# Second layer in three blocks of 512 tokens, the reciprocal kept in h's PSUM bank, and a later start for the first weight conversion

## The chip, the core and the metric

The kernel runs on one core of one Trainium2 chip. The metric is the device time of one execution in microseconds (us), and the figure that is compared is the median over several runs. A profile of one execution lies beside it; times within the profile count from the start of its span.

## The reference

Three stages follow each other. A clustered attention over q, k and v (2 batches, 8 heads, 768 tokens, head size 64) gives 1536 tokens of 512 features; a first layer multiplies them by a 512 x 2048 matrix, applies a leaky rectifier and multiplies by a 2048 x 512 matrix; a second layer does the same with a rational function in the place of the rectifier.

```python
def _attn_ref(q, k, v, centroids):
    ...
    mask = q_assign[:, :, :, None] == k_assign[:, :, None, :]
    scores = scale * np.matmul(q, k.transpose(0, 1, 3, 2))
    scores = np.where(mask, scores, -1000000000.0)
    ...
    return np.matmul(attn, v).astype(np.float32)

def _moe_ref(x, w_in, w_out):
    h = x @ w_in
    g = np.maximum(0.01 * h, h)
    return (g @ w_out).astype(np.float32)

def _moe2_ref(x, w_in, w_out, a, b):
    h = x @ w_in
    h2 = h * h
    h3 = h2 * h
    P = a[0] + a[1] * h + a[2] * h2 + a[3] * h3
    Q = 1.0 + np.abs(b[0]) * np.abs(h) + np.abs(b[1]) * h2
    g = P / (Q + 1e-06)
    return (g @ w_out).astype(np.float32)
```

The weights arrive as 64-bit floats, so each has to be turned into a 32-bit float on the chip before it is used.

## The kernel before, in words

Each fp32 operand is split into a high part (`xh`, `wih`, `woh`, `gh`) and a low part (`xl`, `wil`, `wol`, `gl`), and each product is made of three matmuls: high by high, high by low, low by high.

**Attention** runs in 96 units of 128 query rows (`run`, line 770 and after); a pair of heads has `UP` = 12 units. In the loop's step i, PE transposes the probabilities of unit i-4 (`trans_p`, L627) and then computes the scores of unit i+1 (`scores`, L583); ACT copies the transposed high part (`hi`, L640) and computes the exponential (`exp`, L603); DVE computes the row maximum (`row_max`, L592) and the low part (`lo`, L646); POOL normalizes two units at once in every second step (`normalize`, L619). Pieces that prepare a later pair of heads are put into the same steps by a table (`prep_pieces`): transposes of q and k on PE (`trans`, L243), copies and splits (`split_hi`, L293, and `split_lo`, L298, on POOL), and moves by DMA through SP's queue (`place_a` and `place_b`, L305, out of a tile `hl` with two buffers). The program order is the order on each engine.

Beside the attention runs the conversion of the first layer's first two weight tiles, in tiles called `xst`. In unit 12 their loads are issued on SP's queue (`fill[1].preload(4)`, L885). From unit 15 (`UP + 3`, L846) on, one conversion operation is issued every third unit (`fill[1].step()`): the first is `conv_a` on ACT (L897), which reads the loaded tile, and the two tiles take turns. Then come operations on DVE (L904, L910) and a save (L926).

**The two layers** are one list of steps (n, j, f): n is a group of four tiles of 128 hidden features (the first layer's first group is cut into two of two), j a block of tokens, f the hidden tile within the group. The first layer has 3 blocks of 512 tokens, 48 steps; the second 4 blocks of 384, 64 steps (`width`, L988). A step i does this, in program order:

- `make_h(i)`: 12 matmuls into a PSUM bank `h` (pool `hps`, 4 banks): 4 slices of 128 input features by three products;
- in the second layer, for step i-2: `ratio_recip` on ACT (logarithm `ln`, L1173, and exponential `r`, L1174, which give the reciprocal of the denominator `z`);
- for step i-1: `ratio_act` (ACT writes `y`, the absolute value, L1150, and `u`, L1151; POOL computes `z` in two operations, L1154 and L1157);
- for step i-2: `ratio_end` on DVE (L1180, L1183, L1186), then for step i-1 `ratio_poly` on DVE (L1161, L1162);
- `back`: the matmuls of the output `y` for the steps that `backs(i)` names, into PSUM banks `y0` to `y3` (pool `yps`, 4 banks). In the first layer that is step i-3. In the second, every second step does two at once, i-5 and i-4;
- `next_x`: one piece of the second layer's input is split (ACT L1273, POOL L1274);
- for step i-2: `hi` (ACT, `gh`, L1134) and `lo` (DVE, `gl`, L1139), after which h's bank is free for step i+2;
- `collect`: after the last hidden tile of a block, DVE adds the `y` banks to `acc` in SBUF (L1236) or copies them (L1252); in the second layer's last group the sums are stored by DMA (L1241). In the second layer this comes one step after the `back`, and before `lo`.

`r` of the second layer takes the bank `y3`, since three output banks suffice for 384 tokens. The second layer's input lies in three tiles: `a` (tokens 0 to 767), `b` (768 to 1151) and a tile `c` (the rest), while the first layer used `a` for 1024 tokens and `b` for 512. The lines that matter:

```python
def backs(i):
    ks = [i - LAG] if LAG <= i < M0 + LAG else []
    if i % 2 == 1:
        ks += [k for k in (i - 5, i - 4) if M0 <= k < NS]
    return ks
```

Of the kernel before, what the change touches and what calls it, by code (L numbers as in the profile page):

```python
# [9 lines left out]
F32 = mybir.dt.float32  # L10
# [20 lines left out]
def clustered_attention_moe_moe2(  # L31
# [110 lines left out]
    class Attention:  # L142
# [633 lines left out]
        def run(self, extra, fill):  # L776
# [10 lines left out]
            for i in range(first, NU + TL + 11):  # L787
# [58 lines left out]
                if UP + 3 <= i < NU - 2 * UP and i % 3 == 0:  # L846
                    fill[1].step()
# [140 lines left out]
    def width(m):  # L988
        return 512 if m == 0 else BLK
# [30 lines left out]
    with tc.manual_schedule():  # L1020
# [51 lines left out]
        x1["c"] = [yp.tile([P, NCT, BLK], F32R, name=nm) for nm in ("xhc", "xlc")]  # L1072
# [7 lines left out]
        while weights.waits_for(("wi", 0)):  # L1080
# [3 lines left out]
        LAG = 3  # L1084
        steps = [
            (n, j, f) for n, (m, f0, nf) in enumerate(groups)
            for j in range(NT // width(m)) for f in range(nf)
        ]
        M0 = NG * (NT // width(0)) * NF
# [12 lines left out]
        def tl(nm):  # L1102
            return ew.tile([P, BLK], F32, tag=nm, name=nm)
# [4 lines left out]
        def wide(i):  # L1108
            return width(groups[steps[i][0]][0])

        def make_h(i):
            n, j, f = steps[i]
            wih, wil = weights.get(("wi", n))
            w = wide(i)
            hp = hps.tile([P, 512], F32, tag="h", name="h")[:, 0:w]
            if rational(i):
                (xh, xl), sx = x1["aabc"[j]], slice(j * w if j < 2 else 0, (j * w if j < 2 else 0) + w)
            else:
                (xh, xl), sx = x1["a" if j < 2 else "b"], slice(j % 2 * w, (j % 2 + 1) * w)
# [11 lines left out]
        def hi(i):  # L1131
            d = st[i]
            d["gh"] = gp_.tile([P, 512], F32R, tag="gh", name="gh")[:, 0:wide(i)]
            nc.scalar.copy(d["gh"], d["h"])  # L1134

        def lo(i):
            d = st[i]
            d["gl"] = gp_.tile([P, 512], F32R, tag="gl", name="gl")[:, 0:wide(i)]
            nc.vector.tensor_tensor(d["gl"], d["h"], f32(d["gh"]), op=ALU.subtract)  # L1139
# [26 lines left out]
        def ratio_recip(i):  # L1166
            d = st[i]
            if i == M0:
                r = tl("r")
            else:  # L1170
                r = yps.tile([P, 512], F32, tag="y3", name="r")[:, 0:BLK]
            ln = tl("ln")
            nc.scalar.activation(ln, d["z"], AF.Ln, scale=LNC, bias=lnc)  # L1173
            nc.scalar.activation(r, ln, AF.Exp, bias=lnb, scale=-1.0)  # L1174
            d["r"] = r

        def ratio_end(i):
            d = st[i]
            r = d["r"]
# [16 lines left out]
        def shape(i):  # L1196
            final = rational(i)
            return final, QT if final else NCT, 512

        def back(i):  # L1200
            n, j, f = steps[i]
            nf = groups[n][2]
            final, NO, NW = shape(i)
# [3 lines left out]
            for o in range(NO):  # L1207
                if f == 0:
                    if final and i + nf >= NS and o < 2:
                        cur[o] = hps.tile([P, 512], F32, tag="h", name=f"y{o}")  # L1210
                    else:
                        cur[o] = yps.tile([P, 512], F32, tag=f"y{o}", name=f"y{o}")
# [5 lines left out]
                if i == NS - 1 and o == NO - 1:  # L1218
                    for c in range(2):
                        cs = slice(c * NW // 2, (c + 1) * NW // 2)  # L1220
                        cur[o + 1 + c] = yps.tile([P, 512], F32, tag=f"y{c}", name=f"y{c}")
                        mm3(cur[o + 1 + c][:, 0:NW // 2], [(l, r[:, cs]) for l, r in pairs], True, True)
                else:
                    ends = f == nf - 1 or (i == NS - 2 and o == NO - 1)
                    mm3(cur[o][:, 0:NW], pairs, f == 0, ends)

        def collect(i):
# [4 lines left out]
            final, NO, NW = shape(i)  # L1232
# [5 lines left out]
            def store(o, a, cs=slice(0, NW), queue=nc.sync):  # L1238
                b, t = divmod(j * QT + o, T)
# [7 lines left out]
            if i == NS - 1 - nf or i == NS - 1:  # L1247
                order = [NO - 1] + order[:-1]
            for o in order:
                a = accs[:, (j * NO + o) * NW:(j * NO + o + 1) * NW]  # L1250
# [105 lines left out]
```

## Time and profile before

| | |
|---|---|
| median of 3 runs | 800.63 us (800.05, 800.63, 803.45) |
| profiled execution, its own time | 804.82 us |
| its span, first to last instruction | 803.0 us |
| mean granted TensorE clock | 0.997 of full speed |
| PE (matmul) busy | 782.7 us, 97% |
| DVE, ACT, POOL busy | 82%, 66%, 50% |

The stages in the span: attention to about 270 us, the first layer to about 523 us, the second to the end. A matmul's row shows its modelled duration, which overlaps the next one; the distance from one start to the next is what a matmul takes in a stream. The busy time of an engine counts overlap once. "Granted clock" is the share of full speed that TensorE had in a stretch.

### The profile page before, as it was taken

Reading aid. Unit: us, or ns where it says so; the run is one execution under the profiler, and the core shown is the slowest. Engines: PE = TensorE matmul, PEld = TensorE weight load, DVE = VectorE, ACT = ScalarE, POOL = GpSimd, SP = SyncE. Lnnn points to the kernel's source line nnn. Section 1 sums busy time; section 2 is a strip of 40 time slices with the busy share of each in tenths; the row PEclk is TensorE's granted clock in tenths of the full one; section 3 lists DMA queues with packets and bytes.
Section 4 is the critical chain, followed back from the end, with each engine's and each line's share of the span. In section 5 each row is a group of like instructions: output and inputs, shape, how many; then the busy total and the mean of one; then the engine's idle time right before and its main releaser. Section 6 shows DMA issues by size and latency. Waiting matters only on the chain.

```text
span 803.0 us, 12628 instructions
## 1 busy us (share of the span) xinstructions
PE 782.7 (97%) x4218; PEld 686.2 (85%) x4218; DVE 658.9 (82%) x1202; ACT 527.6 (66%) x1103; POOL 398.9 (50%) x440
## 2 busy tenths in 40 slices
PE   8898999999999999999999999999999999999997
PEld 6697898999888788888888888888899998989996
DVE  7986999988989578877477578768998888888886
ACT  5887988988889554454254246448777667676662
POOL 3875877877675423230041024258656555463441
PEclk9999999999999999999999999999999999999999
DMA  3594662654420233336445444421010101000112
GB/s 101 154 217 99 147 153 75 175 136 94 101 89 1 106 105 129 133 122 220 131 156 184 127 162 129 161 91 40 31 36 27 40 27 40 14 2 0 40 40 79
DMA packets 42112, 78.61 MB, mean 98 GB/s; under 512 B 5248, under 2 KB 25280, under 8 KB 42048
## 3 DMA queue, kind: packets, MB, share of 16 engines
q1 hardware_dynamic: 41760, 77.65, 32.5%
q8 instruction: 33, 0.54, 0.3%
q14 instruction: 31, 0.25, 0.1%
q10 hardware_dynamic: 288, 0.16, 0.1%
HBM read 49.84 MB, written 9.96 MB: 74 GB/s over the span
## 4 chain that ended last, share of the span: by engine, by line
PE 79%; DVE 8%; DMA 4%; ACT 4%; POOL 3%; issue 1%; SPq 0%; DVEq 0%; POOLq 0%; ACTq 0%
PE y L1097 31%; PE h L1097 30%; PE o L663 5%; PE pT L627 5%; PE s L583 5%; DVE pl L646 2%; DVE nm L592 2%; PE sims L326 2%; DMA xst<-in_moe_w_in_dram 1%; ACT ph L640 1%; PE pa L243 1%; POOL e L619 1%; DMA st<-in_moe_w_out_dram 1%; DMA kraw<-in_k_dram 1%; DMA st<-in_moe_w_in_dram 1%
## 5 line engine op out<-in xcount | busy, mean ns | idle before, releaser
L646 DVE TENSOR_TENSOR pl<-pT,ph 128x384 fp32r<-128x384 f32 x192 | 97.2, 546 | 21.0 <-ACT ph L640 20.8
L619 POOL TENSOR_SCALAR e<-e,sum 128x768 f32<-128x768 f32 x96 | 88.6, 935 | 43.1 <-DVE sum L615 31.2
L920 POOL TENSOR_TENSOR wil<-wf,wih 128x512 fp32r<-128x512 f32 x32 | 42.9, 1353 | 128.3 <-ACT wih L917 121.7
L1154 POOL TENSOR_SCALAR z<-y,abv 128x384 f32<-128x384 f32 x64 | 43.1, 674 | 114.8 <-ACT y L1150 114.8
L1139 DVE TENSOR_TENSOR gl<-h,gh 128x384 fp32r<-128x384 f32 (+1 forms) x112 | 67.9, 609 | 35.2 <-ACT gh L1134 35.0
L1097 PE MATMUL h<-xha,wih 128*128 128x512 f32 (+1 forms) x256 | 92.8, 363 | 0.6 <-DVE gl L1139 0.6
L1097 PE MATMUL h<-xha,wil 128*128 128x512 f32 (+1 forms) x256 | 92.8, 362 | 0.0
L1097 PE MATMUL h<-xla,wih 128*128 128x512 f32 (+1 forms) x256 | 92.7, 362 | 0.0
L603 ACT ACTIVATE e<-s,nm 128x768 f32<-128x768 f32 x96 | 87.4, 910 | 7.8 <-DVE nm L592 4.6
L640 ACT CAST ph<-pT 128x384 fp32r<-128x384 f32 x192 | 82.3, 482 | 15.4 <-PE pT L627 13.8
L592 DVE TENSOR_REDUCE nm<-s 128x1 f32<-128x768 f32 x96 | 90.9, 947 | 0.5
L1134 ACT CAST gh<-h 128x384 fp32r<-128x384 f32 (+1 forms) x112 | 59.1, 528 | 41.3 <-DVE h L1186 39.8
L627 PE MATMUL pT<-ident,e 128*128 128x128 f32 x576 | 81.6, 276 | 3.2 <-DVE pl L646 3.1
L910 DVE SCALAR_TENSOR_TENSOR wf<-st,wf 128x512 int32<-128x512 int32 x124 | 80.9, 706 | 0.0
L1097 PE MATMUL y<-woh,gh 128*128 128x512 f32 (+1 forms) x193 | 74.9, 388 | 0.7 <-ACT r L1174 0.7
L1097 PE MATMUL y<-woh,gl 128*128 128x512 f32 (+1 forms) x193 | 75.5, 391 | 0.0
L627 PEld LDWEIGHTS pT<-ident,e 128*128 128x128 f32 x576 | 67.4, 143 | 9.4 <-DVE pl L646 2.6
L1097 PE MATMUL y<-wol,gh 128*128 128x512 f32 (+1 forms) x193 | 75.4, 391 | 0.0
L1097 PE MATMUL y<-gl,woh 128*128 128x512 f32 x192 | 74.9, 390 | 0.1
L1097 PE MATMUL y<-gh,wol 128*128 128x512 f32 x192 | 74.8, 389 | 0.0
L1097 PE MATMUL y<-gh,woh 128*128 128x512 f32 x192 | 74.7, 389 | 0.0
L897 ACT ACTIVATE wf<-st 128x512 f32<-128x512 f32 x62 | 41.4, 669 | 42.3 <-DMA st<-in_moe_w_in_dram 20.5
(131 smaller groups left out, 2045.8 us busy)
## 6 DMA issues: line engine op xcount, KB each, us to landing
st<-in_moe_w_out_dram SPq DMA_DIRECT2D x32, 512.0 KB, 4.4
st<-in_moe_w_in_dram SPq DMA_DIRECT2D x30, 512.0 KB, 4.8
a<-hl SPq DMA_DIRECT2D x56, 192.0 KB, 4.4
b<-hl SPq DMA_DIRECT2D x28, 192.0 KB, 5.7
wf<-scratch_wi SPq DMA_DIRECT2D x14, 256.0 KB, 2.6
qraw<-in_q_dram SPq DMA_DIRECT2D x16, 192.0 KB, 2.8
kraw<-in_k_dram SPq DMA_DIRECT2D x16, 192.0 KB, 3.6
vraw<-in_v_dram SPq DMA_DIRECT2D x8, 384.0 KB, 4.8
```

The costliest lines, as they stand in the source:

```text
L592: nc.vector.reduce_max(un["nm"], un["s"][:, 0:S], axis=AX.X, negate=True)
L603: nc.scalar.activation(un["e"], un["s"][:, 0:S], AF.Exp, bias=un["nm"], accum_out=un["recip"])
L619: nc.gpsimd.tensor_scalar(un["e"], un["e"], un["recip"], 1.0, op0=ALU.mult, op1=ALU.mult)
L627: nc.tensor.transpose(pp[:, kt * P:(kt + 1) * P], un["e"][:, k0:k0 + P], ident)
L640: nc.scalar.copy(un["hi", part], un["pT", part])
L646: nc.vector.tensor_tensor(self.group[gi]["pl"][:, part * n:(part + 1) * n, i * P:(i + 1) * P], un["pT", part], f32(un["hi", part]), op=ALU ...
L910: nc.vector.scalar_tensor_tensor(wi, hold["st", i][:, :, :, 1 - w], sc, wi, op0=op, op1=ALU.bitwise_or)
L920: nc.gpsimd.tensor_tensor(hold["l"][:, i:i + wr, :], hold["wf", i], f32(hold["h"][:, i:i + wr, :]), op=ALU.subtract,)
L1097: nc.tensor.matmul(o, lhsT=l, rhs=r, start=(first and idx == 0), stop=(last and idx == n - 1),)
L1134: nc.scalar.copy(d["gh"], d["h"])
L1139: nc.vector.tensor_tensor(d["gl"], d["h"], f32(d["gh"]), op=ALU.subtract)
L1154: nc.gpsimd.tensor_scalar(d["z"], d["y"], abv[:, 1:2], abv[:, 0:1], op0=ALU.mult, op1=ALU.add)
```

## The change

The second layer gets the first's shape: 3 blocks of 512 tokens, 48 steps, with the input where the first layer had its own (`x_block`; tile `c` is gone). `ratio_recip` writes the reciprocal over `d["h"]`, in h's own bank, and `ratio_end` works there in place; four banks of `y` serve both layers. `backs` gives one step at a time: i-3 for the first layer, i-4 for the second; `collect` follows in the same step, after `lo`. For the very last step the last output tile is made in two halves in banks of `hps`. In attention, `UP + 3` becomes `UP + 6`.

```diff
-                if UP + 3 <= i < NU - 2 * UP and i % 3 == 0:
+                if UP + 6 <= i < NU - 2 * UP and i % 3 == 0:
                     fill[1].step()
...
-    def width(m):
-        return 512 if m == 0 else BLK
+    W = 512
...
-        x1["c"] = [yp.tile([P, NCT, BLK], F32R, name=nm) for nm in ("xhc", "xlc")]
...
         def tl(nm):
-            return ew.tile([P, BLK], F32, tag=nm, name=nm)
+            return ew.tile([P, W], F32, tag=nm, name=nm)
...
+        def x_block(j):
+            return x1["aab"[j]], slice(j % 2 * W, (j % 2 + 1) * W)
...
         def ratio_recip(i):
             d = st[i]
-            if i == M0:
-                r = tl("r")
-            else:
-                r = yps.tile([P, 512], F32, tag="y3", name="r")[:, 0:BLK]
             ln = tl("ln")
             nc.scalar.activation(ln, d["z"], AF.Ln, scale=LNC, bias=lnc)
-            nc.scalar.activation(r, ln, AF.Exp, bias=lnb, scale=-1.0)
-            d["r"] = r
+            nc.scalar.activation(d["h"], ln, AF.Exp, bias=lnb, scale=-1.0)
...
             nc.vector.scalar_tensor_tensor(
-                d["h"], r, -2.0, d["u"], op0=ALU.add, op1=ALU.mult
+                r, r, -2.0, d["u"], op0=ALU.add, op1=ALU.mult
             )
 
         def backs(i):
-            ks = [i - LAG] if LAG <= i < M0 + LAG else []
-            if i % 2 == 1:
-                ks += [k for k in (i - 5, i - 4) if M0 <= k < NS]
-            return ks
+            return [k for k in (i - LAG, i - LAG - 1) if 0 <= k < NS and rational(k) == (k < i - LAG)]
...
                 if f == 0:
-                    if final and i + nf >= NS and o < 2:
-                        cur[o] = hps.tile([P, 512], F32, tag="h", name=f"y{o}")
-                    else:
-                        cur[o] = yps.tile([P, 512], F32, tag=f"y{o}", name=f"y{o}")
+                    cur[o] = yps.tile([P, W], F32, tag=f"y{o}", name=f"y{o}")
...
         def next_x():
             j, o, a = later.pop(0)
...
+            (xh, xl), sx = x_block(j)
+            nc.scalar.copy(xh[:, o, sx], a)
+            nc.gpsimd.tensor_tensor(xl[:, o, sx], a, f32(xh[:, o, sx]), op=ALU.subtract)
...
-            for k in backs(i - 1):
-                if rational(k):
-                    collect(k)
             for k in backs(i):
                 back(k)
             if later:
                 next_x()
...
             for k in backs(i):
-                if not rational(k):
-                    collect(k)
+                collect(k)
```

Three places of the program, as instructions in order. First ACT in attention, before, around the first conversion operation (`xst`), where `sum` is the end of unit 15 and the `ph` behind it belongs to the next step:

```order
L603 ACTIVATE e,sum<-s,nm 128x768
L610 ACTIVATE sum<-sum,eps 128x2
L897 ACTIVATE xst<-xst 128x512
L640 CAST ph<-pT 128x3x128 x2
L246 ACTIVATE x<-pa 128x384
```

And the same stretch of ACT now:

```order
L603 ACTIVATE e,sum<-s,nm 128x768
L610 ACTIVATE sum<-sum,eps 128x2
L640 CAST ph<-pT 128x3x128 x2
L246 ACTIVATE x<-pa 128x384
L603 ACTIVATE e,sum<-s,nm 128x768
L640 CAST ph<-pT 128x3x128 x2
L246 ACTIVATE x<-pa 128x384
L603 ACTIVATE e,sum<-s,nm 128x768
L610 ACTIVATE sum<-sum,eps 128x2
L640 CAST ph<-pT 128x3x128 x2
L676 COPY tmp<-o 64x384
L603 ACTIVATE e,sum<-s,nm 128x768
L897 ACTIVATE xst<-xst 128x512
```

The operation on `xst` stands three units (three exponentials) later; nothing else of ACT moved there.

Second, DVE at the end of a block in the middle of the second layer, before (`acc<-y` is the collection of three output tiles, `gl` the low part, the rows that read `r` are `ratio_end`, the two that write `u` from `h` are `ratio_poly`):

```order
L1186 SCALAR_TENSOR_TENSOR h<-r,u 128x384
L1161 TENSOR_TENSOR u<-u,h 128x384
L1162 SCALAR_TENSOR_TENSOR u<-u,nav,h 128x384
L1236 TENSOR_TENSOR acc<-y_7241,acc 128x512
L1236 TENSOR_TENSOR acc<-y_7245,acc 128x512
L1236 TENSOR_TENSOR acc<-y_7249,acc 128x512
L1139 TENSOR_TENSOR gl<-h,gh 128x384
L1180 SCALAR_TENSOR_TENSOR u<-u,nav,r 128x384
```

And now:

```order
L1176 SCALAR_TENSOR_TENSOR h<-h,u 128x512
L1156 TENSOR_TENSOR u<-u,h 128x512
L1157 SCALAR_TENSOR_TENSOR u<-u,nav,h 128x512
L1134 TENSOR_TENSOR gl<-h,gh 128x512
L1217 TENSOR_TENSOR acc<-y_6861,acc 128x512
L1217 TENSOR_TENSOR acc<-y_6865,acc 128x512
L1217 TENSOR_TENSOR acc<-y_6869,acc 128x512
L1217 TENSOR_TENSOR acc<-y_6873,acc 128x512
L1170 SCALAR_TENSOR_TENSOR u<-u,nav,h 128x512
L1173 SCALAR_TENSOR_TENSOR h<-z,h 128x512
```

The collection stands behind `gl`, has four tiles, and follows its matmuls in the same step; `r` has become `h` in `ratio_end`.

Third, ACT where the second layer begins, now (the exponential L1165 writes `h` where it wrote `r`; `xha<-acc` is the split of the second layer's input):

```order
L1145 ACTIVATE y<-h 128x512
L1146 ACTIVATE u<-h,nav 128x512
L1250 CAST xha<-acc 128x512
L917 CAST wih<-wf 128x512
L1164 ACTIVATE ln<-z,lnc 128x512
L1165 ACTIVATE h<-ln,lnb 128x512
```

Before, a piece of the split was two instructions (of 256 and 256, or 128 and 384 tokens); now it is one of 512, and the exponential's output stands in the bank that `ratio_poly` has read.

## Rows read from the trace of the kernel before

**Rows 1.** The page's busy line: time, share of the span and instructions of each engine.

```profile
PE 782.7 (97%) x4218; PEld 686.2 (85%) x4218; DVE 658.9 (82%) x1202; ACT 527.6 (66%) x1103; POOL 398.9 (50%) x440
```

**Rows 2.** Waits of PE, the longest: who for whom, total us, times, longest.

```profile
PE pa L243 <- DVE pl L646: 3.2, 1, 3.2
```

**Rows 3.** Stretches of first and second layer: length, busy us per engine, granted clock, DMA.

```profile
440.00:480.00 40.00, 40.00 (x179) 33.11 (x178) 24.41 (x39) 15.69 (x27) 5.55 (x4) 1.00 0.47 158
600.00:640.00 40.00, 40.00 (x204) 36.44 (x203) 34.56 (x65) 28.29 (x54) 22.49 (x25) 1.00 0.09 31
```

**Rows 4.** The same view, three stretches of attention (order: PE, PEld, DVE, ACT, POOL).

```profile
58.00:62.00 4.00, 2.23 (x14) 1.73 (x14) 1.91 (x4) 1.01 (x4) 2.77 (x4) 1.00 1.07 282
62.00:66.00 4.00, 2.61 (x14) 2.32 (x15) 3.22 (x7) 4.00 (x10) 0.93 (x1) 0.80 1.06 227
66.00:70.00 4.00, 4.00 (x24) 3.81 (x24) 2.61 (x6) 2.58 (x7) 2.24 (x3) 0.78 0.63 138
```

**Rows 5.** Timeline of ACT, units 15 to 18: start, duration, instruction, wait before it.

```profile
57.44 0.90 ACT L603 ACTIVATE e<-s,nm 128x768 f32<-128x768 f32 x1
...
61.72 0.66 ACT L897 ACTIVATE xst<-xst 128x512 f32<-128x512 f32 x1 [2.96 <-DMA xst<-in_moe_w_in_dram]
...
69.54 0.90 ACT L603 ACTIVATE e<-s,nm 128x768 f32<-128x768 f32 x1
```

**Rows 6.** Timeline of POOL in the same stretch.

```profile
67.76 0.83 POOL L293 TENSOR_SCALAR hl<-x 128x768 fp32r<-128x768 f32 x1 [4.83 <-DMA a<-hl]
68.57 1.80 POOL L619 TENSOR_SCALAR e<-e,sum 128x768 f32<-128x768 f32 x2
```

**Rows 7.** Timeline of PE in the same stretch.

```profile
63.39 0.55 PE L243 MATMUL pa<-ident,kraw 128*128 128x128 f32 x3 [3.17 <-DVE pl L646]
...
73.59 0.82 PE L627 MATMUL pT<-ident,e 128*128 128x128 f32 x6
```

**Rows 8.** Timeline of PE in the first layer, matmuls number 1 and 241 of a stretch.

```profile
397.49 0.39 PE L1097 MATMUL h<-xha,wih 128*128 128x512 f32 x1
...
451.89 0.39 PE L1097 MATMUL h<-xhb,wih 128*128 128x512 f32 x1
```

**Rows 9.** Chain that ended last, second layer: start, us, line, count (pairs 1 and 26).

```profile
566.17 4.18 PE h L1097 x24
570.35 4.12 PE y L1097 x18
...
773.84 4.18 PE h L1097 x24
```

**Rows 10.** Timeline of PE where the second layer begins.

```profile
541.22 0.34 PE L1097 MATMUL h<-xha,wil 128*128 128x384 f32 x1
542.13 0.45 PE L1097 MATMUL h<-xha,wih 128*128 128x384 f32 x1 [0.57 <-DVE gl L1139]
...
560.76 0.34 PE L1097 MATMUL h<-xhb,wil 128*128 128x384 f32 x1
561.81 0.47 PE L1097 MATMUL y<-woh,gh 128*128 128x512 f32 x1 [0.71 <-ACT r L1174]
```

**Rows 11.** Groups of DVE, shapes apart, 300 to 500 us: count, busy us, mean ns.

```profile
L1139 DVE TENSOR_TENSOR gl<-h,gh 128x512 fp32r<-128x512 f32 x37 | 25.2, 686 | 22.9 <-ACT gh L1134 22.8
```

**Rows 12.** The same view, 566 to 790 us, and ACT's there.

```profile
L1139 DVE TENSOR_TENSOR gl<-h,gh 128x384 fp32r<-128x384 f32 x55 | 30.3, 550 | 0.0
L1236 DVE TENSOR_TENSOR acc<-y,acc 128x512 f32<-128x512 f32 x30 | 18.8, 682 | 0.0
L1173 ACT ACTIVATE ln<-z,lnc 128x384 f32<-128x384 f32 x54 | 33.4, 618 | 9.4 <-POOL z L1157 8.5
L1174 ACT ACTIVATE r<-ln,lnb 128x384 f32<-128x384 f32 x55 | 32.2, 586 | 1.8
```

**Rows 13.** Timeline of DVE and PE at the end.

```profile
795.20 0.56 DVE L1139 TENSOR_TENSOR gl<-h,gh 128x384 fp32r<-128x384 f32 x1 [0.60 <-ACT gh L1134]
796.61 2.71 DVE L1236 TENSOR_TENSOR acc<-y,acc 128x512 f32<-128x512 f32 x5 [0.85 <-PE y L1097]
```

More of the change, by code (lines that the diff above doesn't have):

```diff
@@ L1084, in clustered_attention_moe_moe2 @@
         LAG = 3
+        NO = W // P
         steps = [
             (n, j, f) for n, (m, f0, nf) in enumerate(groups)
-            for j in range(NT // width(m)) for f in range(nf)
+            for j in range(NT // W) for f in range(nf)
         ]
-        M0 = NG * (NT // width(0)) * NF
+        M0 = NG * (NT // W) * NF
         NS = len(steps)
@@ L1113, in make_h @@
             wih, wil = weights.get(("wi", n))
[L1114 to L1117, printed above, removed]
-            else:
-                (xh, xl), sx = x1["a" if j < 2 else "b"], slice(j % 2 * w, (j % 2 + 1) * w)
+            hp = hps.tile([P, W], F32, tag="h", name="h")
+            (xh, xl), sx = x_block(j)
             sl = slice(f * P, (f + 1) * P)
@@ L1132, in hi @@
             d = st[i]
-            d["gh"] = gp_.tile([P, 512], F32R, tag="gh", name="gh")[:, 0:wide(i)]
+            d["gh"] = gp_.tile([P, W], F32R, tag="gh", name="gh")
             nc.scalar.copy(d["gh"], d["h"])
@@ L1137, in lo @@
             d = st[i]
-            d["gl"] = gp_.tile([P, 512], F32R, tag="gl", name="gl")[:, 0:wide(i)]
+            d["gl"] = gp_.tile([P, W], F32R, tag="gl", name="gl")
             nc.vector.tensor_tensor(d["gl"], d["h"], f32(d["gh"]), op=ALU.subtract)
@@ L1219, in back @@
                     for c in range(2):
-                        cs = slice(c * NW // 2, (c + 1) * NW // 2)
-                        cur[o + 1 + c] = yps.tile([P, 512], F32, tag=f"y{c}", name=f"y{c}")
-                        mm3(cur[o + 1 + c][:, 0:NW // 2], [(l, r[:, cs]) for l, r in pairs], True, True)
+                        cs = slice(c * W // 2, (c + 1) * W // 2)
+                        cur[NO + c] = hps.tile([P, W], F32, tag="h", name="yh")
+                        mm3(cur[NO + c][:, 0:W // 2], [(l, r[:, cs]) for l, r in pairs], True, True)
                 else:
                     ends = f == nf - 1 or (i == NS - 2 and o == NO - 1)
-                    mm3(cur[o][:, 0:NW], pairs, f == 0, ends)
+                    mm3(cur[o], pairs, f == 0, ends)
         def collect(i):
@@ L1236, in add, with store @@
                 nc.vector.tensor_tensor(a, y, a, op=ALU.add)
-            def store(o, a, cs=slice(0, NW), queue=nc.sync):
-                b, t = divmod(j * QT + o, T)
+            def store(o, a, cs=slice(0, W), queue=nc.sync):
+                b, t = divmod(j * NO + o, T)
                 t = tile_of(t)
@@ L1246, in collect @@
             order = list(range(NO))
-            if i == NS - 1 - nf or i == NS - 1:
+            if i == NS - 1:
                 order = [NO - 1] + order[:-1]
             for o in order:
-                a = accs[:, (j * NO + o) * NW:(j * NO + o + 1) * NW]
+                a = accs[:, (j * NO + o) * W:(j * NO + o + 1) * W]
                 if first:
-                    nc.vector.tensor_copy(a, cur[o][:, 0:NW])
+                    nc.vector.tensor_copy(a, cur[o])
                 else:
-                    add(cur[o][:, 0:NW], a)
+                    add(cur[o], a)
                 if last and not final:
@@ L1259, in collect @@
             if i == NS - 1:
-                a = accs[:, (j * NO + NO - 1) * NW:(j * NO + NO) * NW]
+                a = accs[:, (j * NO + NO - 1) * W:(j * NO + NO) * W]
                 for c in range(2):
-                    cs = slice(c * NW // 2, (c + 1) * NW // 2)
-                    add(cur[NO + c][:, 0:NW // 2], a[:, cs])
+                    cs = slice(c * W // 2, (c + 1) * W // 2)
+                    add(cur[NO + c][:, 0:W // 2], a[:, cs])
                     store(NO - 1, a, cs, (nc.sync, nc.scalar)[c])
@@ L1267, in next_x @@
             j, o, a = later.pop(0)
[L1268 to L1274 removed]
+            (xh, xl), sx = x_block(j)
+            nc.scalar.copy(xh[:, o, sx], a)
+            nc.gpsimd.tensor_tensor(xl[:, o, sx], a, f32(xh[:, o, sx]), op=ALU.subtract)
         later = []
@@ L1280, in load_step @@
             weights.step(max(0, due - (total - weights.pending())))
-        for i in range(NS + LAG + 3):
+        for i in range(NS + LAG + 1):
             if i < NS and steps[i][1:] == (0, 0):
```

21 lines of the change are left out of this document (4 added, 17 removed).

## The prediction

> **What bounds the kernel now.** I read the busy line of the page first. PE works 97% of the span [rows 1], so time is won only where PE stands idle, runs slowly, or needs less time for the same columns. The table by stretches then shows the layers apart from the rest: PE is busy in all 40 us of a stretch of either layer, at full granted clock, while DVE has 61% of the time in the first layer and 86% in the second [rows 3]. Shorter waits inside the layers' steady part are therefore worth nothing; only the distance from one matmul to the next counts. The list of PE's waits shows where it is idle: one wait of 3.2 us stands alone at the top [rows 2]. Its place is in attention near 60 us, and there the granted clock falls as well, to 0.80 and 0.78, which means that part of that time ran at 1.2 in place of 2.4 GHz [rows 4]. Two more waits lie where the second layer begins [rows 10]. The change touches exactly these: the width in the second layer, its beginning, its end, and the spot in attention.
>
> **The second layer's steady part.** In the first layer 240 matmuls of 512 columns take 451.89 - 397.49 = 54.40 us, 0.2267 us each [rows 8]. In the second, 24 of 384 columns take 4.18 us, 0.1742 each, and 18 of 512 columns 4.12 us, 0.2289 each [rows 9]. Twenty-five pairs of steps take 773.84 - 566.17 = 207.67 us, 8.31 us a pair, with no gap. So 128 columns more cost 0.0525 us, and a matmul has a fixed part of some 0.017 us that does not shrink with its width; where widths alternate, the 512-column ones are also 0.0022 us slower than in the first layer.
>
> The change keeps the columns and makes 64 x 12 = 768 matmuls of `h` into 48 x 12 = 576. By these rows `h` falls from 768 x 0.1742 = 133.8 us to 576 x 0.2267 = 130.6 us: 3.2 us. The 576 matmuls of `y` stay, and if all widths are equal each saves 0.0022 us: 1.3 us. By pairs the sum is 32 x 8.31 = 265.9 against 48 x 24 x 0.2267 = 261.2 us. I take 4.6 us. The bounds are 3.2 (the slower `y` was not due to the mixing) and 4.7.
>
> The Trainium skill (TensorE: Matmul & The Clock Gate, section Back-to-back issue gap) gives the warm distance as columns over 2.4 GHz plus 2.5 ns, so that 192 matmuls fewer would be worth 0.5 us, by an estimate from that page. The rows above have 0.2267 us where that gives 0.216, and I hold with the rows.
>
> **Does PE stay fed at 512?** A step now takes PE 24 x 0.2267 = 5.44 us. The old step took 4.15 us, in which DVE was busy 34.56 us in 40, or 3.59 us a step [rows 3], 0.51 of it the three collected tiles per four steps (0.682 each, rows 12). Scaled by 4/3 the rest is at most 4.1 us, and four collected tiles add 0.68: 4.8 us, 88% of a step. One row has the same operation at both widths: `gl` goes from 550 to 686 ns, by 1.25 [rows 11, 12], so 4.8 is the high end. ACT (28.29 us in 40, now at most 3.9 us a step) and POOL (3.1) have more room. So I cost the wider work at nothing; PE covers it. The cover is 0.6 us a step, and if DVE needs more than 5.44 us a step, the excess falls on PE 48 times.
>
> The collection loses its step of delay: DVE must clear bank `y0` before the next block's first `y`. Between lie 12 matmuls of `h`, 2.7 us, and the four adds can follow PE bank by bank, 0.68 us each, so the last ends 0.7 us after PE leaves it. Behind them on DVE waits `ratio_end` of the next step, and behind that the low part that PE needs two steps, 11 us, later. Nothing.
>
> The reciprocal now overwrites `h`, so the exponential (ACT) must wait for `ratio_poly` of its own step (DVE). Queued behind it on ACT are the absolute value and `u` of the next step. On DVE `gl` of the step before, 0.69 us, lies between `ratio_poly` and the first reader of the reciprocal; the exponential takes 0.59 us at 384 and at most 0.78 at 512 [rows 12]. That hides all but a tenth of a microsecond, inside the 0.6 spare. The in-place reading of a PSUM bank is already done on `r` today, so it has no new price. Nothing.
>
> **Where the second layer begins.** PE stands twice: 542.13 - 541.22 - 0.17 = 0.74 us and 561.81 - 560.76 - 0.17 = 0.88 us [rows 10], 1.6 us. The first is a bank of `h` whose low part is late, the sixth step of the second layer. That step starts 18.8 us after the layer's first now, and 24.5 us after it with 512 columns and single `y` steps, while the chain behind it grows by less than 2 us. The second ends when DVE clears `y` banks after a pair of blocks' steps; it will have its 2.7 us. The exponential no longer waits for bank `y3`, and the input's split has 24 instructions on ACT and POOL together in place of 40. Gain 1.6 us, bounds 0 and 1.6.
>
> **The end.** Now PE's last matmuls are followed by adds of DVE and the stores [rows 13]; that stays, with four tiles for three, three of them cleared while PE still works. New is the order before it: after the last `h`, PE has four steps of `y`, 48 x 0.2267 = 10.9 us, and needs the last low part 0.45 us later, at 11.3. DVE first collects a block, which ends at 2.7 + 0.7 = 3.4 us, and then has ten operations to the last `gl`: 10 x 0.69 = 6.9 us at the price of rows 11, and 0.6 of waiting for `gh` as now [rows 13]: 10.9 us. It fits with 0.4 us to spare; if the operations with two constants scale by the full 4/3 it is about a microsecond late. I take a loss of 0.5 us, bounds 0 and 1.
>
> Sum for the second layer: 4.6 + 1.6 - 0.5 = 5.7 us.
>
> **The spot in attention.** ACT waited 2.96 us, to 61.72, for the load of `xst` [rows 5]; everything behind it on ACT, the copies `ph` first, came late, then DVE's `pl`, then PE, idle for 3.17 us [rows 7]. The slow clock cost (1 - 0.80) x 4 + (1 - 0.78) x 4 = 1.7 us of PE's time more [rows 4]. Together 4.9 us. Three units later the operation stands behind the exponential that now starts at 69.54 [rows 5]; without the stall that one comes some 5 us earlier, at about 64.7, ends at 65.5, and the load has been there since 61.7. So the wait goes.
>
> What is late next is POOL: it waited 4.83 us, to 67.76, for a DMA that frees `hl`, and only then normalizes units 16 and 17, from 68.57 [rows 6]. That DMA does not come earlier because ACT does. PE's transposes of unit 16 now start at 73.59 [rows 7]; they can't start before the first normalization ends, 68.57 + 0.90 = 69.5. So 4.1 of the 4.9 us can be kept. The other conversion operations move by three units too, so they stand at the same places of a unit. The two saves on SP's queue pass eight moves out of `hl`; their data are complete two turns of the tile before, so nothing behind them waits. Nothing.
>
> In the profiled execution the sum is 5.7 + 4.1 = 9.8 us: 804.82 - 9.8 = 795.0. That execution is 4.2 us above the median of the runs, and the runs spread by 3.4. The landing of a load in heavy traffic is what can differ from run to run, so the median run may have a smaller stall. I take 3.0 us for it there, ACT's own wait [rows 5], between 0 and 4.9: 800.63 - 5.7 - 3.0 = **791.9 us**.
>
> **Rivals.**
> - *Attention gives nothing in the median* (chance 0.24): the stall is the profiled execution's own, or POOL's wait on the DMA of `hl` [rows 6] takes its place whole. For it speaks the 4.2 us between profile and median. 800.63 - 5.7 = 794.9.
> - *The fixed part of a matmul is not saved* (0.05): `h` then costs as much per column as before, and 3.2 us drop out: 795.1. Rows 8 and 9, with both widths in one trace, speak against it. It is the outcome that the page of the Trainium skill named above comes near to.
> - *DVE sets the pace* (0.06): the exponential is not hidden behind `gl`, because ACT reaches logarithm and exponential only after `ratio_poly`. A step on DVE is then 4.8 us plus the two at 4/3 of 0.62 and 0.59 [rows 12], 1.6: 6.4, and 48 x (6.4 - 5.44) = 46 us are lost: 800.63 - 8.7 + 46 = 838. It decides from a step of 5.44 us on, and outweighs the gain from 5.62. Against it: `z` is ready long before, and the logarithm needs nothing else.
> - *Smaller gains, no change that can be told* (0.05): the beginning keeps its waits and the end loses a microsecond, with nothing from attention: 800.63 - 4.6 + 1 = 797.0.
>
> **Numbers.** The forecast has 0.60. Its own range is 789.0 to 794: the low end has the whole of attention and no loss at the end, 800.63 - 6.2 - 4.9 = 789.5, with half a microsecond of run to run. The first two rivals carry the range up to 796.6. A measurement of this kernel can tell about 0.5%, 4 us. Faster than 796.6: the forecast, most of the first two rivals, 0.84. Same: 0.10. Slower: 0.06.
>
> **What would show it.** Right: in the second layer, starts of matmuls 0.2267 us apart and steps of 5.44 us; no wait of PE over 0.3 us between its first and last step; DVE's share below 90%; no wait of ACT on `xst`, and the granted clock at 1.00 near 60 us, with a PE wait of about a microsecond in front of unit 16. Wrong: a wait of PE for `gl` or `acc` in every block, a step longer than 5.44 us, or the 3 us stall found again at another place of attention.

## The result, and the profile after

The changed kernel takes 794.46 us (median of 6 runs, 793.58 to 794.83), the kernel before 800.76 (6 runs, 799.92 to 804.02) beside it. The ratio is 0.9911, its 95% interval 0.9891 to 0.9932: faster, and clear of the 0.5% that the prediction took as the least that can be told. The forecast was 791.9, so the sign is right and the point is 2.6 us too low. 794.46 lies half a microsecond above the forecast's own range (789.0 to 794) and inside the wider one up to 796.6, which its first two rivals carry; it is the first rival's 794.9 that the time comes nearest to. The new profiled execution takes 794.29 us, its span 792.2, at a granted clock of 1.000. The two profiled executions thus differ by 804.82 - 794.29 = 10.5 us, where the prediction's sum had 9.8. The medians differ by 6.3, where it had 8.7. What is to be explained is this gap between profile and median.

The page's busy line after, which answers to [rows 1]:

```profile
PE 775.4 (98%) x4026; PEld 658.6 (83%) x4026; DVE 646.2 (82%) x1106; ACT 510.7 (64%) x1015; POOL 387.8 (49%) x400
```

The 192 matmuls are gone (4218 to 4026), and so are 96 instructions of DVE and 88 of ACT. PE is now busy for 98% of a shorter span.

The table by stretches after: three pieces of attention (against [rows 4]) and two of the second layer (against [rows 3]):

```profile
58.00:62.00 4.00, 4.00 (x27) 3.44 (x27) 3.97 (x8) 3.79 (x9) 2.77 (x4) 1.00 1.09 243
62.00:66.00 4.00, 4.00 (x33) 3.90 (x32) 3.78 (x8) 3.74 (x10) 0.14 (x2) 1.00 1.10 209
66.00:70.00 4.00, 3.87 (x27) 3.34 (x27) 3.08 (x7) 3.52 (x11) 4.00 (x5) 1.00 0.70 142
560.00:600.00 40.00, 40.00 (x179) 33.11 (x178) 34.31 (x52) 26.47 (x43) 21.21 (x20) 1.00 0.10 34
600.00:640.00 40.00, 40.00 (x178) 33.15 (x177) 35.29 (x54) 26.66 (x44) 23.20 (x22) 1.00 0.12 40
```

Near 60 us PE worked 2.23 and 2.61 us of 4 before, at a clock down to 0.78. Now it works all of the time, at 1.00. In the second layer 178 or 179 matmuls stand in 40 us where 204 stood; DVE is busy 34.3 and 35.3 us, 86 and 88%.

The longest waits of PE after (us in total, times, longest), where [rows 2] had the wait for `pa` at the top:

```profile
PE pT L627 <- DVE pl L646: 3.4, 7, 1.1
PE s L583 <- ACT e L603: 2.6, 8, 0.7
```

The 3.2 us before `pa` are gone, and between 500 and 790 us no wait of PE is left at all, so those of [rows 10] are gone as well. The chain that ended last, from the last steps of the first layer to the last `h`:

```profile
531.92 2.72 PE y L1096 x12
534.64 5.44 PE h L1096 x24
540.08 2.72 PE y L1096 x12
...
771.28 2.72 PE h L1096 x12
```

Twelve matmuls take 2.72 us without a break, so a step takes 5.44 us and a matmul 0.2267, as in the first layer [rows 8]. The 24 `h` at 534.64 are the one place where a step has no `y`, because `y` then comes one step later.

### The profile page after: what moved, and what is told of

Read it like the earlier page. It is cut to its first block, busy times and chain, and to the rows that moved or that the text cites. A ratio compares the mean times of both kernels' runs of the same rounds, so it can differ in the third digit from the quotient of the medians.

```text
span 792.2 us, 11944 instructions
## 1 busy us (share of the span) xinstructions
PE 775.4 (98%) x4026; PEld 658.6 (83%) x4026; DVE 646.2 (82%) x1106; ACT 510.7 (64%) x1015; POOL 387.8 (49%) x400
## 4 chain that ended last, share of the span: by engine, by line
PE 83%; DVE 9%; POOL 3%; ACT 3%; issue 1%; DMA 0%; DVEq 0%; POOLq 0%; ACTq 0%
PE h L1096 33%; PE y L1096 31%; PE o L663 5%; PE s L583 5%; PE pT L627 4%; DVE pl L646 3%; DVE nm L592 3%; PE sims L326 2%; POOL e L619 2%; ACT ph L640 1%; PE pa L243 1%; ACT e L603 1%; DVE acc L1217 1%; POOL xla L703 0%; DVE sv L357 0%
## 5 line engine op out<-in xcount | busy, mean ns | idle before, releaser
L1129 ACT CAST gh<-h 128x512 fp32r<-128x512 f32 x96 | 56.4, 588 | 69.4 <-DVE h L1176 67.9
L1096 PE MATMUL h<-xha,wil 128*128 128x512 f32 x256 | 99.6, 389 | 0.0
L1096 PE MATMUL h<-xla,wih 128*128 128x512 f32 x256 | 99.6, 389 | 0.0
L1096 PE MATMUL h<-xha,wih 128*128 128x512 f32 x256 | 99.6, 389 | 0.0
L1134 DVE TENSOR_TENSOR gl<-h,gh 128x512 fp32r<-128x512 f32 x96 | 65.6, 686 | 35.7 <-ACT gh L1129 35.4
L1149 POOL TENSOR_SCALAR z<-y,abv 128x512 f32<-128x512 f32 x48 | 37.0, 771 | 117.3 <-ACT y L1145 117.3
L603 ACT ACTIVATE e<-s,nm 128x768 f32<-128x768 f32 x96 | 87.3, 910 | 8.7 <-DVE nm L592 4.1
L1217 DVE TENSOR_TENSOR acc<-y,acc 128x512 f32<-128x512 f32 x84 | 56.7, 690 | 28.4 <-PE y L1096 28.1
L1096 PE MATMUL y<-woh,gl 128*128 128x512 f32 x191 | 74.4, 390 | 0.0
L1096 PE MATMUL y<-wol,gh 128*128 128x512 f32 x191 | 74.3, 389 | 0.0
L1096 PE MATMUL y<-woh,gh 128*128 128x512 f32 x191 | 74.3, 389 | 0.0
```

The costliest lines, as they stand in the source:

```text
L603: nc.scalar.activation(un["e"], un["s"][:, 0:S], AF.Exp, bias=un["nm"], accum_out=un["recip"])
L1096: nc.tensor.matmul(o, lhsT=l, rhs=r, start=(first and idx == 0), stop=(last and idx == n - 1),)
```

## Where the two executions differ

The start of the first `h` of each layer and of the last matmul cut each profiled execution into three stages. The first stage varies; the other two do not.

| kernel | attention (first `h` at) | first layer | second layer |
|---|---|---|---|
| before, as shown | 269.17 | 253.4 | 275.75 |
| before, again (third experiment) | 265.19 | 253.0 | 275.69 |
| after | 264.82 | 253.3 | 269.34 |
| after, again (its second profile, below) | 265.24 | 253.3 | 269.33 |

The second layer gives 6.4 us in any pair of profiles. In attention the profile of before that the prediction rests on was 4.0 us later than a second profile of the same kernel, while the change is only 0.4 us earlier than that second one, and its own second profile not at all. My theory from here: the whole of the 6.3 us comes from the second layer, and the stall near 60 us is in the median run a small one. The rival: the stall is as large in every run, and something else in attention takes its gain.

## Experiments

### The two halves of the change, apart

The second layer alone is the change with the conversion left where it was:

```diff
-                if UP + 6 <= i < NU - 2 * UP and i % 3 == 0:
+                if UP + 3 <= i < NU - 2 * UP and i % 3 == 0:
```

> The new layers with the old start of the conversion (unit 15). Theory A (the stall in attention costs 3 us in the usual run): 5.7 to 6.4 us below before, so 794.4 to 795.1, but some 3 us above the full change, which would then stand near 791.5. Theory B (the stall of the profiled execution is missing in the usual run): the full change's 794.5 in the usual run, and now and then a run that is 3 to 5 us longer, as before has (803.45 and 804.02 among 799.9 to 800.9). In the profile the second layer takes 269.2 us from its first h to its last matmul, as in the full change.

Measured: 794.41 us (6 runs, 793.19 to 796.48) against 800.8 for before (21 runs, 799.2 to 805.12), ratio 0.992 (0.9902 to 0.9937). That is the full change's time, without its attention part. In its profile ACT waits 1.89 us for `xst` and PE 2.2 us before `pa`, with the granted clock at 1.00. Here too the profiled execution is the slowest of its six, 2.1 us above their median.

The conversion alone is the kernel before with the opposite edit (`UP + 6`):

> The old layers with the conversion from unit 18 on. Theory A: 3 us below before, 797.7. Theory B: before's usual 800.2 in all runs, without the long ones near 803.5 to 804; in the profile no wait of ACT on xst, and a span some 4 to 5 us below the 803.0 of the profile of before.

Measured: 800.41 us (12 runs, 799.19 to 802.41), ratio to before 0.9995 (0.998 to 1.001). The wait for `xst` is gone from its profile (span 799.6), and 0.4 us remain in the median, within the uncertainty. The 797.7 that a stall of 3 us in every run would give lies outside the interval. Both of the second layer's first waits are still there.

The kernel before, once more with a profile:

> The kernel before, unchanged, for a second profile. Theory A: the wait of ACT on xst near 3 us again, granted clock below 0.85 near 64 us, span near 803. Theory B: a wait under 1 us or none, granted clock 1.00 there, span near 798 to 799.

Measured: 800.32 us, span 798.5. Its ACT row of the first conversion operation, from the timeline, and its stretch at 58 us:

```profile
59.37 0.68 ACT L897 ACTIVATE xst<-xst 128x512 f32<-128x512 f32 x1 [1.26 <-DMA xst<-in_moe_w_in_dram]
```

```profile
58.00:62.00 4.00, 2.44 (x17) 2.04 (x17) 2.41 (x6) 2.73 (x8) 3.14 (x4) 1.00 1.08 235
```

The same load makes ACT wait 1.26 us here where it was 2.96 [rows 5], PE stands 1.6 us before `pa` in place of 3.17, and the clock does not fall: PE is idle for less time. The loss of clock belongs to the long stall only.

A fourth profile of the early start has no stall at all. It is that of the kernel before with `r` in SBUF (under "The reciprocal's place"), whose attention is unchanged:

```profile
63.18 0.66 ACT L897 ACTIVATE xst<-xst 128x512 f32<-128x512 f32 x1
```

In these four profiles (before, again, second layer alone, `r` in SBUF) the load landed 9.9, 8.0, 8.5 and 7.9 us after its issue, near 52 us each time. In the last one ACT came to unit 15 only at 61.96 us, where it came at 56.8 to 57.4 in the others, because attention had lost 4.6 us between units 2 and 8; the load had landed by then, at 59.91. So the stall is what is left between ACT's arrival and the landing, and it ran from nothing to 2.96 us in four executions.

### Is a wait at this place worth its length?

Had the stall been covered by something else, its size would not matter. This puts the first operation into unit 12, right behind the issue of the load:

```diff
-                if UP + 6 <= i < NU - 2 * UP and i % 3 == 0:
+                if UP <= i < NU - 2 * UP and i % 3 == 0:
```

> The full change, but the first conversion operation in unit 12, in the unit that issues its load. The load needs 5 to 10 us, so ACT must wait in every run. If such a wait goes through to the end of the program, the time rises by the wait less some 1 to 2 us that the buffers between ACT and PE cover, and by up to 2 us for a slower clock: 5 to 10 us above the full change, 800 to 804. If waits of ACT there are covered (a rival in which even the profiled stall cost nothing), it stays at 794.5.

Measured: 803.66 us (8 runs), ratio to before 1.0033 (1.0021 to 1.0046), 9.2 us above the full change. The same ACT row, PE's wait and three stretches of its profile:

```profile
59.75 0.66 ACT L897 ACTIVATE xst<-xst 128x512 f32<-128x512 f32 x1 [9.17 <-DMA xst<-in_moe_w_in_dram]
```

```profile
PE pa L243 <- DVE pl L646: 9.3, 2, 9.1
```

```profile
54.00:58.00 4.00, 0.00 (x0) 0.00 (x0) 0.00 (x0) 0.00 (x0) 0.00 (x0) 0.69 1.06 241
58.00:62.00 4.00, 0.57 (x3) 0.57 (x4) 1.19 (x3) 2.25 (x5) 0.00 (x0) 0.50 1.08 264
62.00:66.00 4.00, 4.00 (x18) 3.77 (x17) 3.64 (x7) 2.96 (x8) 3.56 (x4) 0.53 0.50 115
```

A wait of 9.2 us makes the run 9.2 us longer, against the full change. That the two agree so closely is partly chance: in its profile units 12 to 18 lose 11.6 us, wait and slow clock together, and part of that comes back by unit 42 (table below). PE falls to half clock while it stands, and works at 0.53 for about 4 us after the others have resumed. So little of such a wait is hidden, and the chain from ACT to PE that the prediction named is right. What was wrong is its size in the median run.

Two more starts of the conversion, in unit 17 and from unit 42 on:

```diff
-                if UP + 6 <= i < NU - 2 * UP and i % 3 == 0:
+                if i == UP + 5 or UP + 6 <= i < NU - 2 * UP and i % 3 == 0:
```

> The full change, but the first conversion operation (conv_a on ACT) in unit 17 and the others three units earlier than in the full change, so that DVE's conversion operations stand in the units where before has them. Theory C (of the 1.8 us that the vanished wait gives by unit 18, about 1.0 is given back by unit 42, because DVE's conversion operations moved into a stretch where DVE is the pace): no wait on xst, and 0.5 to 1.0 us below the full change, 793.5 to 794.0. Rival (it is given back whatever the place of DVE's operations, since DVE's own work sets the pace from unit 20 to 42): 794.4, the same as the full change, within 0.2.

Measured: 794.08 us (4 runs, 793.79 to 795.81), ratio 0.9915 (0.990 to 0.993): not to be told from the full change, and no wait for `xst`. It lies between the two forecasts, and its units 12 to 42 take 75.95 us, where two profiles of the full change have 76.96 and 75.69: it decides neither for the place of DVE's operations nor against it.

```diff
-                if UP + 6 <= i < NU - 2 * UP and i % 3 == 0:
+                if UP + 30 <= i < NU - 2 * UP:
```

> The full change with the whole conversion of the first tiles in units 42 to 59, one operation in each unit, where PE and not DVE is the pace. If DVE's conversion operations cost time in units 18 to 42 because DVE is full there: units 12 to 42 take 75 to 75.7 us (for 76.96), units 42 to 95 stay at 129.1, and the time is 1 to 1.5 us below the full change, 793. If it is not their place that counts: units 12 to 42 stay near 76.5 to 77, and 794.4. If they fill DVE in the new place as well: units 42 to 95 grow by 0.5 to 2 us.

Measured: 795.31 us (5 runs, 794.67 to 796.34), ratio 0.9936 (0.9922 to 0.9949). The times between the starts of ACT's exponentials (L603) show where it loses, in us from one unit to another:

| profile | ACT's wait for `xst` | units 12 to 18 | 18 to 42 | 42 to 95 |
|---|---|---|---|---|
| before, as shown | 2.96 | 19.10 | 61.31 | 129.19 |
| before, again | 1.26 | 15.91 | 61.29 | 129.07 |
| second layer alone | 1.89 | 16.54 | 61.71 | 129.05 |
| conversion alone | none | 14.15 | 62.32 | 129.06 |
| full change | none | 14.30 | 62.66 | 129.08 |
| full change, again | none | 14.16 | 61.54 | 129.13 |
| from unit 42 on | none | 14.51 | 59.37 | 132.31 |
| from unit 12 on | 9.17 | 25.85 | 61.19 | 129.07 |
| from unit 17 on | none | 14.98 | 60.97 | 129.04 |
| start at unit 18, `h` in halves | none | 14.16 | 64.06 | 129.12 |
| start at unit 18, `y` three steps behind | none | 14.17 | 62.19 | 129.09 |
| start at unit 18, `r` in SBUF | none | 14.24 | 61.54 | 129.03 |
| start at unit 15, `r` in SBUF | none | 14.69 | 61.12 | 129.26 |

The last four rows are of runs described below that change only the layers.

The last column but one matters: without any conversion beside them, units 18 to 42 take 59.4 us, with it 61.0 to 64.1, and the run from unit 42 on pays the difference later (132.3 in place of 129.1). So none of its three cases came as stated: the conversion costs attention some 2 to 3 us in either place. Against an ordinary stall, a later start removes 1.6 to 2.4 us up to unit 18 (15.91 and 16.54 against 14.15 to 14.30). In the next 24 units the six profiles that start at unit 18 take 61.5 to 64.1 us, 62.4 on average, and the four that start at unit 15 take 61.1 to 61.7, 61.4 on average: about 1 us is given back, with a wide spread. DVE is busy for 22.94 of the 24 us from 86 to 110 us in the full change; that this is the cause was not shown.

The full change once more:

> The full change, unchanged, beside the later conversion on the same chip: 794.4, and a second profile of it, with no wait on xst and 269.3 us for the second layer.

Measured: 794.74 us (5 runs, 794.58 to 795.85), ratio 0.9929 (0.9916 to 0.9941), the profiled execution's span 792.5, no wait for `xst`, and 269.33 us for the second layer, as expected.

### What a matmul costs beside its columns

`h` of the second layer in two halves of 256 columns: the same columns, 576 more matmuls.

```diff
-            mm3(hp, pairs, True, True)
+            for c in range(2):
+                cs = slice(c * W // 2, (c + 1) * W // 2)
+                if rational(i):
+                    mm3(hp[:, cs], [(l, r[:, cs]) for l, r in pairs], True, True)
+                elif c == 0:
+                    mm3(hp, pairs, True, True)
```

> The full change with the second layer's h made of twice as many matmuls of 256 columns: 1152 for 576. By the trace of before (0.118 us between matmuls of 256 columns at its end, 0.2267 of 512) the layer is 1152 x 0.118 - 576 x 0.2267 = 5.4 us longer, 274.6 us from first h to last matmul. If a matmul's fixed part were 2.5 ns (the Trainium skill, TensorE: Matmul & The Clock Gate, section Back-to-back issue gap) it would be 576 x 0.0025 = 1.4 us longer, 270.6.

Measured: 804.42 us, the second layer 277.94 us against 269.34, with no wait of PE in it. A step in its chain of waits:

```profile
643.92 2.75 PE y L1096 x12
646.67 2.87 PE h L1096 x24
```

The 24 halves take 2.87 us where 12 whole ones take 2.72, and `y`, unchanged, takes 2.75 beside them. So 576 matmuls more cost 277.94 - 269.34 = 8.6 us. Of that, 0.15 us a step or 7.2 us is `h`'s own, 12.5 ns for each matmul more, and 0.03 us a step or 1.4 us is the slower `y`. Both expected times are too short: the 5.4 us because a matmul of 256 columns takes 0.1197 us here and not 0.118, and because `y` was left out. The prediction's 17 ns is a third too high, and the other case's 2.5 ns a fifth of what was measured.

### The reciprocal's place

What does it cost the old kernel that `r` lies in the bank `y3`? This edit gives it a tile in SBUF at every step, as before only at the first:

```diff
-            if i == M0:
+            if True:
                 r = tl("r")
```

> The kernel before with the reciprocal always in a tile of SBUF, not in bank y3. If bank y3 caused the two waits of PE where the second layer begins (0.74 and 0.88 us), both are gone and the second layer is 1.6 us shorter, 274.0 from first h to last matmul for 275.6. If the backlog of POOL and the late collection of the y banks cause them, the first goes, and the second stays near 0.8: 274.8. If neither: 275.6.

Measured: 861.22 us. Where I expected a gain of 1.6 us, 60 us were lost. DVE's groups of `ratio_end` in its second layer (580 to 830 us), and one of them beside POOL in the timeline:

```profile
L1186 DVE SCALAR_TENSOR_TENSOR h<-r,u 128x384 f32<-128x384 f32 x49 | 53.4, 1091 | 1.7
L1183 DVE SCALAR_TENSOR_TENSOR r<-z,r 128x384 f32<-128x384 f32 x50 | 45.6, 913 | 5.9 <-DVE u L1180 0.5
L1180 DVE SCALAR_TENSOR_TENSOR u<-u,nav,r 128x384 f32<-128x384 f32 x50 | 37.2, 744 | 5.9 <-ACT r L1174 2.3
```

```profile
704.69 1.19 POOL L1157 TENSOR_TENSOR z<-z,y 128x384 f32<-128x384 f32 x1
705.04 1.26 DVE L1186 SCALAR_TENSOR_TENSOR h<-r,u 128x384 f32<-128x384 f32 x1
```

With `r` in PSUM these three took 566, 555 and 612 ns on average. Now they take 1091, 913 and 744. Sorted by what POOL does meanwhile, the first takes 0.57 us where POOL stands (12 times) and 1.26 where it works (37 times); with `r` in PSUM it takes 0.57 in either case. DVE becomes the bound: 37.28 of 40 us from 640 to 680 us, with PE at 36.25 and a clock of 0.91.

The same edit in the changed kernel, `r` in a tile of its own in SBUF:

```diff
-            ln = tl("ln")
+            ln, d["r"] = tl("ln"), tl("r")
...
-            nc.scalar.activation(d["h"], ln, AF.Exp, bias=lnb, scale=-1.0)
+            nc.scalar.activation(d["r"], ln, AF.Exp, bias=lnb, scale=-1.0)
...
-            r = d["h"]
+            r = d["r"]
...
-                r, r, -2.0, d["u"], op0=ALU.add, op1=ALU.mult
+                d["h"], r, -2.0, d["u"], op0=ALU.add, op1=ALU.mult
```

> The full change with the reciprocal in a tile of SBUF of its own, so that its exponential need not wait for the polynomial. If only the wait counts: 794.4, as the full change. If the operands' place sets the duration on DVE, as the old layers with r in SBUF showed (913, 1091 and 744 ns at 384 for 555, 566 and 612): 4/3 of 1.0 us more on DVE in each step, 1.35 us, so a step of 4.7 + 1.35 = 6.0 us or a little more for 5.44, and 48 x 0.6 to 48 x 1.0 more: 822 to 842. This is also the price of the rival in which DVE sets the pace.

Measured: 824.79 us, within what was expected. DVE's two costliest groups there (580 to 800 us), the stretch, and PE's longest wait:

```profile
L1176 DVE SCALAR_TENSOR_TENSOR h<-r,u 128x512 f32<-128x512 f32 x36 | 51.4, 1427 | 1.2
L1173 DVE SCALAR_TENSOR_TENSOR r<-z,r 128x512 f32<-128x512 f32 x36 | 38.7, 1074 | 4.0
```

```profile
600.00:640.00 40.00, 35.54 (x156) 28.83 (x155) 38.56 (x46) 21.86 (x37) 24.71 (x19) 1.00 0.10 33
```

```profile
PE y L1096 <- DVE acc L1217: 19.0, 8, 4.5
```

The same two groups of the full change, 560 to 770 us, where the reciprocal lies in h's bank:

```profile
L1176 DVE SCALAR_TENSOR_TENSOR h<-h,u 128x512 f32<-128x512 f32 x40 | 28.0, 699 | 1.4
L1173 DVE SCALAR_TENSOR_TENSOR h<-z,h 128x512 f32<-128x512 f32 x40 | 27.6, 690 | 0.0
L1134 DVE TENSOR_TENSOR gl<-h,gh 128x512 fp32r<-128x512 f32 x39 | 26.7, 684 | 0.0
```

1427 and 1074 ns stand against 699 and 690: 1.1 us more a step. With it DVE is at 38.56 of 40 us, PE waits for the collection, and the second layer loses what the width gained and more. The step of 5.44 us needs the reciprocal in a bank of PSUM.

### Is the fourth step of delay for y needed?

```diff
-            return [k for k in (i - LAG, i - LAG - 1) if 0 <= k < NS and rational(k) == (k < i - LAG)]
+            return [k for k in (i - LAG,) if 0 <= k < NS]
...
-        for i in range(NS + LAG + 1):
+        for i in range(NS + LAG):
```

> The full change with y of the second layer three steps behind h, as in the first, not four. If the fourth step is needed for the end alone: no wait of PE in the steady part, and PE waits 2.3 to 2.8 us for the last gl at the end, less 0.1 of now: 797. If DVE's order needs it in the steady part too: waits of PE for gl in many steps, and more than 5 us longer, above 799.5. If it is not needed at all: 794.4.

Measured: 795.5 us (4 runs, 795.23 to 796.36), ratio 0.9927 (0.991 to 0.9944); the second layer takes 270.82 us, 1.5 more. Its only waits in that layer, from PE's timeline:

```profile
783.97 0.50 PE L1096 MATMUL y<-woh,gl 128*128 128x512 f32 x1 [0.41 <-DVE gl L1134]
786.89 0.50 PE L1096 MATMUL y<-woh,gh 128*128 128x512 f32 x1 [0.36 <-ACT gh L1129]
```

So the steady part and the beginning need only three steps, and the fourth pays at the end, 1.5 us in the profile and about a microsecond in the median. PE waits there for the low part of the last step but one and for the high part of the last. I had expected 2.3 to 2.8 us, for the last low part.

## Why the prediction was right, and where not

**The steady part: right.** Taken 4.6, bounds 3.2 and 4.7. From 518.32 to 774.00 us the chain has 94 pieces of 2.72 us, 48 steps make 261.1 us against 265.8 by the 25 pairs before (207.67 / 25 x 32, [rows 9]; the prediction's 265.9 is rounded up): 4.7 us, the upper bound. The 0.0022 us that `y` took more beside 384 columns are gone; they are there again beside 256 (2.75 us for twelve in place of 2.72). The fixed part of a matmul, "some 0.017 us", came out at 12.5 ns as the price of one `h` matmul more. With this the Trainium skill (TensorE: Matmul & The Clock Gate, section Back-to-back issue gap) does not agree: its 2.5 ns would make 1.4 us of the 7.2 by which `h` grew with 576 more matmuls. Holding with the rows was right.

**The beginning: right.** Both waits of [rows 10] are gone, 1.6 us, and with the 4.7 us, less 0.1 at the end, they make 6.2 of the layer's 6.4 us. Which edit removes them is open. It is not the fourth step, as the run without it shows. The test of the bank `y3` was swamped by its side effect.

**The end: mis-sized, 0.5 taken, 0.1 measured.** The timeline of DVE and PE at the end of the full change:

```profile
773.84 0.39 PE L1096 MATMUL y<-woh,gh 128*128 128x512 f32 x1
...
784.43 0.69 DVE L1134 TENSOR_TENSOR gl<-h,gh 128x512 fp32r<-128x512 f32 x1 [0.71 <-ACT gh L1129]
785.18 0.50 PE L1096 MATMUL y<-woh,gl 128*128 128x512 f32 x1
785.51 0.39 PE L1096 MATMUL y<-woh,gh 128*128 128x512 f32 x1
```

The low part ends at 785.12, PE begins at 785.18, and its next matmul comes 0.33 us later in place of 0.23. Counted from the first `y` behind the last `h`, at 773.84, the low part took 11.3 us, all of the 11.3 that I had allowed, so nothing of the 0.4 us was to spare. The ten operations took 7.0 us without the wait for `gh`: they scaled as `gl` does, not by 4/3.

**DVE and the exponential: right, and close.** DVE's 86 to 88% are the 88% of the prediction. The exponential is hidden but for a wait of `ratio_end`, 6.6 us over 40 steps, 0.17 each, where "a tenth" was said (560 to 770 us):

```profile
L1170 DVE SCALAR_TENSOR_TENSOR u<-u,nav,h 128x512 f32<-128x512 f32 x40 | 29.8, 745 | 6.6 <-ACT h L1165 6.6
```

The rival in which DVE sets the pace did not occur, but DVE can set it, for another reason than the rival's: in the run with `r` in SBUF, DVE needs about 1.1 us more a step, the 0.6 us of cover are gone, and 30 us are lost.

**Attention: the term that failed.** The step is "I take 3.0 us for it there, ACT's own wait". Removing the wait worked in the profile as said. This is the stretch after, ACT, POOL and PE:

```profile
64.86 0.67 ACT L897 ACTIVATE xst<-xst 128x512 f32<-128x512 f32 x1
65.96 0.83 POOL L293 TENSOR_SCALAR hl<-x 128x768 fp32r<-128x768 f32 x1 [3.86 <-DMA a<-hl]
66.77 1.79 POOL L619 TENSOR_SCALAR e<-e,sum 128x768 f32<-128x768 f32 x2
67.93 0.82 PE L627 MATMUL pT<-ident,e 128*128 128x128 f32 x6
```

The operation stands where it was forecast, without a wait. The transposes of unit 16 start 73.59 - 67.93 = 5.66 us earlier [rows 7]; 0.77 of that was there at unit 12 already, and 4.9 are the stall. One sub-step was wrong, "That DMA does not come earlier": it freed `hl` at 65.96 in place of 67.76 [rows 6], so POOL kept nothing back, and no wait of a microsecond stands before unit 16. In the second profile of before, which has a stall, it freed `hl` at 65.56, so the 67.76 is not owed to the early operation as such. Of the 4.8 us by unit 18, 1.35 are given back by unit 42 (62.66 against 61.31). That the profiled sum of 9.8 comes near 10.5 is thus partly luck: 0.7 more from the second layer (6.4 for 5.7), 0.7 more from the stall (4.8 for 4.1) and the 0.77 us that were there before stand against the 1.35 given back.

In the median almost nothing is left: 0.4 us from the conversion alone (interval -0.8 to 1.6), none from the full change against the second layer alone (794.46 and 794.74 against 794.41, with intervals of 1.0 to 1.7 us to either side). The stall of the profiled execution was an unusually long one, 3.2 us longer up to unit 18 than in the second profile, a fourth profile had none, and about 1 us of what an ordinary one costs is given back by unit 42. The prediction had the clue and used 1.1 us of it (3.0 in place of 4.1): a profiled execution 4.2 us above the median, with one stall of 4.9 us in it. Had it put the whole of the 4.2 on that stall, 0.7 would have been left, and with the second layer's 5.7 the forecast would have been 794.2. The rival "Attention gives nothing in the median", 794.9, is what happened, by the first of its two reasons; its second (POOL's wait takes the place of the stall) fell.

**What stays open.** How long the stall is in executions without a profile cannot be seen. The runs of before reach to 805.1 (3 of the 21 beside the first experiments lie above 802.5), those of the full change (11 runs) to 795.85, so the change may mainly cut off the long cases. The number of runs is too small to show it, and long cases need not come from this stall: in the profile of before with `r` in SBUF, attention had lost 4.6 us by unit 8, without any wait for `xst`. What exactly gives the time back between units 18 and 42 was not isolated.

## What to carry to other kernels

A stall in one profiled execution is that execution's: before a term is taken from it, set the execution's own time against the median, and put the excess on the stall first, above all if it is a DMA's landing. A stream without gaps repeats to a tenth of a microsecond between profiles, and there a distance from start to start, read at two widths, prices a change of tiling well. Where an engine has 12% to spare, an operand's place in SBUF or PSUM may decide over that margin, so such a move is costed on the engine that reads the operand, beside what the other engines do at that time.

## What the runs showed of the hardware that was not expected

- A DVE instruction of 128 x 384 with both inputs in SBUF took 1.26 us beside a working POOL and 0.57 us without; with one input in PSUM, 0.57 us in either case. With the other two of `ratio_end` it cost 60 us of 800 in the old kernel and 30 in the new (one run each). The Trainium skill (SBUF — State Buffer, section Who interferes with whom) says that such an instruction contends with a GpSimd one that reads SBUF, and that one with at most one SBUF input, outside the 2-port modes, does not. The trace agrees: 1.26 us and 0.57 us. POOL was slowed less, 1.19 us for `z` in the row above and 1.02 beside `r` in PSUM.
- A matmul of 512 columns was slower among matmuls of another width: 0.2289 us beside 384 [rows 9] and 0.229 beside 256 (2.75 for 12), 0.2267 among its like. What causes it was not tried.
- The same load, issued at the same place of the program, landed 7.9 to 9.9 us after its issue in four profiles of the early start, and made ACT wait for nothing, 1.26, 1.89 and 2.96 us.
